# Attention followed by a three-way maximum layer on one core: the row maxima turned in five blocks of 116 columns in place of six of 96

## The chip, the cores and the metric

The kernel runs on 1 core of one Trainium2 chip. Its time is what the device takes for one execution, in microseconds (us). Before the change it was 1497.14 us, the median of 3 runs (1493.35 to 1499.3). A core has five engines that run side by side: TensorE (PE in the profile, with its weight loads shown apart as PEld), VectorE (DVE), ScalarE (ACT), GpSimd (POOL) and SyncE (SP), which issues DMA transfers.

## The reference

Everything is float32: 8 batches, 8 heads, 1152 keys, head size 64.

```python
q_pool = q.reshape(B, H, S // 2, 2, D).mean(axis=3)     # 576 queries
scores = scale * np.matmul(q_pool, k.transpose(0, 1, 3, 2))
scores = scores - np.max(scores, axis=-1, keepdims=True)
attn = np.exp(scores)
attn = attn / (np.sum(attn, axis=-1, keepdims=True) + 1e-09)
out = np.matmul(attn, v)
# x: 4608 tokens x 512, the heads of one token side by side
h = np.maximum(np.maximum(x @ w1, x @ w2), x @ w3)      # 4608 x 768
y = h @ w_out                                           # 4608 x 512
```

## The kernel before, in words

**Units.** The attention part is cut into 64 units, numbered 0 to 63: 8 batches, 4 pairs of heads, 2 halves of the queries. A unit holds 288 queries of each of two heads, 576 columns in all, side by side, against 1152 keys in 9 blocks of 128. Keys are on the partitions, queries along the columns.

**One unit, step by step.** For each of the 9 key blocks TensorE writes scores for both heads into `pqk` (L495 and L496, each half of a split float32 product), ScalarE copies them to the tile `s` (L501), and VectorE keeps a running maximum `acc`, 128 partitions x 2 heads x 288 queries (L507, L510). There are two score buffers, so the products of one block wait for the copy and the maximum of the block two before. The maximum of a query over the 128 partitions that are left is found per head: TensorE turns `acc` by three transposes of 96 columns into `pmt` (step "rows", L543), VectorE reduces that to `m`, 96 partitions x 3 (step "red", L549), and TensorE spreads `m` over all 128 partitions by three more transposes into `pmb` (step "bc", L556), 96 columns each. Per unit that makes six transposes of each sort. Then VectorE subtracts `pmb` from `s` in six instructions, one for each three key blocks and head (L571, 864 elements per partition), ScalarE takes the exponential of the same six pieces (L577), GpSimd adds the key blocks to `ksum` (L590, L592), and TensorE multiplies with the values into `pav` (L620) and sums the keys (L634, or L651 and L666 in units 0 to 15).

**The last layer.** The 4608 tokens are cut into nine chunks, most of 512 columns. A chunk is 216 matmuls into `ph` (L882, three matrices, each float32 product as three matmuls) and 72 into `po` (L937). Chunk 0 begins when the first batch is through and runs among the units of later batches. With it the weights, which come as 64-bit floats, are converted (tile `w64`, L782 to L815, mostly VectorE); the other chunks read the converted weights back. So units 0 to 8 have attention alone, those after them carry chunk 0 and conversions, and the later ones carry a steady share of chunks. The last two chunks and what is left of the one before run after the last unit.

**The order.** Nothing is scheduled at run time. Every step is put on a list with the engine it needs, what it must follow and a cost in us, such as `[pe(400)]` for the three transposes of "rows". The function `arrange` walks through a plan of time: whichever engine is free next takes, among the steps that are ready, the one with the lowest rank. The rank is the unit's number plus a number for the sort of step (table `RANK`) plus a number for the sort of step and the unit (table `NUDGE`, for names such as `sub.3`). What comes out is a fixed order of instructions on each engine, and semaphores hold an instruction until its inputs are there.

Of the kernel before, what the change touches and what calls it, by code (L numbers as in the profile page):

```python
# [9 lines left out]
F32 = mybir.dt.float32  # L10
# [12 lines left out]
QH = 288  # L23
DM = 512
# [11 lines left out]
    "qk": -64.087414,  # L36
    "cp": -201.632297,
    "mx": -98.140426,
    "rows": -272.840782,
    "red": -68.635955,  # L40
    "bc": -93.634816,
    "sub": 4.726236,
    "exp": -213.793739,
    "keys": -56.547354,
    "av": 20.056295,
    "xcopy": -255.632957,
    "psum": 357.906867,
    "eps": 37.531305,
    "inv": 376.584889,
    "xm": -67.169839,  # L50
    "load": -24.04249,
    "prep": 419.666386,
    "move": 224.230816,
    "split": 23.71928,
    "ffn": -28.691504,
    "rate": 0.892435,
    "mm": 52.75274,
    "fetch": -99.724728,
    "evac": -190.100398,
    "hhigh": 126.204061,  # L60
    "hlow": -167.886807,
    "conv": 378.084906,
    "rate0": 3.367239,
    "first_qk": 72.728419,
    "first_cp": -178.421168,
    "first_mx": 23.500417,
    "first_sub": 91.32154,
    "first_exp": 338.912979,
    "first_keys": 32.988795,
    "first_av": 60.682988,  # L70
    "first_xcopy": -140.422607,
    "first_psum": -82.473329,
    "first_inv": -18.571991,
    "first_xm": -117.084517,
    "first_load": -319.235449,
    "first_prep": -243.969765,
    "first_move": -391.229363,
    "first_split": 131.799961,
# [163 lines left out]
def pe(n):  # L242
    return ("pe", n * 1e-3)
# [15 lines left out]
def tile_attention_ffn(  # L259
# [214 lines left out]
    def scores(d, n, half):  # L474
# [7 lines left out]
        for kk in range(NK):  # L482
            apart = d < APART and kk % 3 == 2
            for hs in [(0, 1), (1, 2)] if apart else [(0, 2)]:
# [44 lines left out]
                if kk:  # L529
                    after = [c] + ([copies[0]] + (old.rows if old else []) if kk == 1 else [tops[-1]])  # L530
                    x = step("mx", r, [dve(n * QH)], top, after, give="ff" if apart else None)
                    tops.append(x)
                if not apart:
                    uses.append([c, x])

        o.rows, o.subs, o.exps, o.pt, o.pb, o.m = [], [[], []], {}, {}, {}, {}
        pools = (ps_a, ps_b)
        for h in range(2):

            def rows(e, h=h):  # L540
                o.pt[h] = pools[h].tile([P, 512], F32, tag="ab"[h], name=f"pmt{d}_{h}")
                for i in range(3):
                    nc.tensor.transpose(  # L543
                        o.pt[h][:96, i * P : (i + 1) * P], o.acc[:, h, 96 * i : 96 * i + 96], ident
                    )
# [476 lines left out]
```

## Time and profile before

| | us |
|---|---|
| median of 3 runs | 1497.14 |
| the profiled execution, its own time | 1492.46 |
| its span, first to last instruction | 1490.6 |
| PE busy | 1407.2 (94%) |
| POOL busy | 1076.9 (72%) |
| DVE busy | 1054.8 (71%) |
| ACT busy | 906.5 (61%) |

The profile shows one execution. "Busy" is the time in which an engine has an instruction under way; matmuls overlap and their ends are modelled, so the time by which one matmul holds up the next is read from how far the end of a run of them moves with each one more, not from the length of one. The granted TensorE clock (PEclk) is 1.00 where the chip grants 2.4 GHz and 0.50 where it grants 1.2 GHz; a stretch with some of both has a value in between.

### The profile page before, as it was taken

What the parts mean: (1) busy time and instruction counts of PE and PEld (TensorE: products, weight loads), DVE (VectorE), ACT (ScalarE), POOL (GpSimd) and SP (SyncE); (2) the same over time, 40 slices, a digit from 0 to 9 for tenths busy, and PEclk for the clock granted to TensorE, in tenths of its full rate; (3) what the DMA queues carried; (4) which work ended last, traced back from release to release, by engine and by line L of the source; (5) the groups of instructions that cost most, each with busy time, mean ns of one, the idle gap of its engine ahead of it and who ended that gap; (6) DMA issues with size and microseconds to landing.
All of it is one profiled execution on the core that took longest, in us unless ns stands there. A gap on an engine that the chain in (4) does not pass through costs nothing.

```text
span 1490.6 us, 24961 instructions
## 1 busy us (share of the span) xinstructions
PE 1407.2 (94%) x8832; PEld 1114.8 (75%) x8832; DVE 1054.8 (71%) x1441; ACT 906.5 (61%) x1464; POOL 1076.9 (72%) x835
## 2 busy tenths in 40 slices
PE   4889898897899999999999999999999999999999
PEld 4556676775777778777777877777777777778998
DVE  4798788898867777777678777777787778750110
ACT  4777656576666676667666776667667766641211
POOL 1888875689578887789978896788888978680210
PEclk9889899897799999999999999999999999999999
DMA  6565446574356755566466755665566546334441
GB/s 186 155 182 160 128 147 225 160 219 139 110 153 169 210 152 151 174 186 184 119 185 181 197 145 166 188 186 156 169 181 183 152 137 177 109 100 164 156 161 58
DMA packets 114763, 240.73 MB, mean 161 GB/s; under 512 B 15440, under 2 KB 75216, under 8 KB 114640
## 3 DMA queue, kind: packets, MB, share of 16 engines
q1 hardware_dynamic: 114064, 238.55, 54.7%
q8 instruction: 71, 1.16, 0.3%
q10 hardware_dynamic: 576, 0.59, 0.2%
q14 instruction: 52, 0.43, 0.1%
HBM read 144.70 MB, written 18.87 MB: 110 GB/s over the span
## 4 chain that ended last, share of the span: by engine, by line
PE 68%; POOL 2%; DVE 1%; DMA 1%; issue 1%; ACT 1%; SPq 0%; ACTq 0%; POOLq 0%
PE ph L882 26%; PE pav L620 12%; PE po L937 10%; PE pqk L495 7%; PE pqk L496 7%; PE pmt L543 2%; PE psum L634 2%; PE pmb L556 2%; POOL ksum L592 1%; DMA qq<-qraw 1%; DVE s L571 0%; DMA qraw<-in_qT_dram 0%; DVE acc L510 0%; DMA kraw<-in_kT_dram 0%; SPq L425 0%
## 5 line engine op out<-in xcount | busy, mean ns | idle before, releaser
L592 POOL TENSOR_TENSOR ksum<-ksum,s 128x576 f32<-128x576 f32 x448 | 638.0, 1424 | 25.2 <-ACT s L577 3.9
L882 PE MATMUL ph<-xh,w 128*128 128x512 f32 (+2 forms) x1440 | 458.4, 375 | 4.1 <-DVE w L815 2.4
L501 ACT COPY s<-pqk 128x576 f32<-128x576 f32 x576 | 360.8, 636 | 131.8 <-PE pqk L496 128.4
L495 PE MATMUL pqk<-qq,kc 128*128 128x288 f32 x1152 | 360.6, 329 | 57.7 <-DVE acc L510 35.3
L510 DVE TENSOR_TENSOR acc<-acc,pqk 128x576 f32<-128x576 f32 x448 | 334.2, 746 | 113.6 <-ACT s L501 110.7
L571 DVE TENSOR_TENSOR s<-s,pmb 128x864 f32<-128x864 f32 x384 | 393.1, 1045 | 11.2 <-PE pmb L556 11.2
L577 ACT ACTIVATE s<-s 128x864 f32<-128x864 f32 x384 | 352.2, 929 | 52.0 <-DVE s L571 48.4
L496 PE MATMUL pqk<-qq,kc 128*128 128x288 f32 x1152 | 334.2, 305 | 0.0
L495 PEld LDWEIGHTS pqk<-qq,kc 128*128 128x128 f32 x1152 | 226.9, 197 | 112.2 <-DVE acc L510 45.2
L620 PE MATMUL pav<-s,v 128*64 128x288 f32 x2304 | 305.7, 418 | 2.8 <-ACT s L577 2.6
L882 PEld LDWEIGHTS ph<-xh,w 128*128 128x128 f32 x1440 | 263.1, 188 | 42.7 <-issue 3.2
L882 PE MATMUL ph<-xl,w 128*128 128x512 f32 (+2 forms) x720 | 267.7, 372 | 0.0
L620 PEld LDWEIGHTS pav<-s,v 128*64 128x64 f32 x2304 | 166.3, 140 | 119.9 <-issue 14.6
L496 PEld LDWEIGHTS pqk<-qq,kc 128*128 128x128 f32 x1152 | 229.5, 199 | 10.1
L590 POOL TENSOR_TENSOR ksum<-s 128x576 f32<-128x576 f32 x64 | 91.9, 1436 | 134.8 <-ACT s L577 134.3
L913 POOL TENSOR_TENSOR h_lo<-hm,h_hi 128x512 fp32r<-128x512 f32 (+2 forms) x60 | 70.8, 1180 | 136.2 <-ACT h_hi L910 134.1
L903 DVE TENSOR_TENSOR hm<-hm,ph 128x512 f32<-128x512 f32 (+2 forms) x120 | 75.4, 629 | 127.9 <-PE ph L882 126.6
L549 DVE TENSOR_REDUCE m<-pmt 96x3 f32<-96x384 f32 x128 | 68.7, 551 | 108.5 <-PE pmt L543 108.3
L882 PEld LDWEIGHTS ph<-xl,w 128*128 128x128 f32 x720 | 135.8, 189 | 12.9
L391 POOL TENSOR_TENSOR kraw<-kraw 128x1152 fp32r<-128x1152 f32 x31 | 82.6, 2665 | 49.2 <-ACT kraw L387 48.6
L629 ACT COPY xr<-pav 128x288 f32<-128x288 f32 x64 | 25.5, 398 | 132.1 <-PE pav L620 131.9
L641 DVE RECIPROCAL rs<-rs 128x288 f32<-128x288 f32 (+1 forms) x64 | 96.4, 1506 | 9.4 <-ACT rs L638 8.9
(57 smaller groups left out, 1313.7 us busy)
## 6 DMA issues: line engine op xcount, KB each, us to landing
w<-w_split SPq DMA_DIRECT2D x144, 512.0 KB, 3.4
kc<-kraw SPq DMA_DIRECT2D x384, 96.0 KB, 2.6
qq<-qraw SPq DMA_DIRECT2D x252, 144.0 KB, 3.8
v<-in_vr_dram SPq DMA_DIRECT2D x32, 576.0 KB, 4.0
kraw<-in_kT_dram SPq DMA_DIRECT2D x31, 576.0 KB, 5.0
qraw<-in_qT_dram SPq DMA_DIRECT2D x31, 576.0 KB, 4.7
w<-in_win_dram SPq DMA_DIRECT2D x18, 512.0 KB, 5.5
w_split<-w SPq DMA_DIRECT2D x18, 512.0 KB, 4.4
```

Source lines behind the costliest of these rows:

```text
L495: nc.tensor.matmul(ps[:, h - hs[0], :QH], w, qq[:, 0, h], start=True, stop=False)
L496: nc.tensor.matmul(ps[:, h - hs[0], :QH], w, qq[:, 1, h], start=False, stop=True)
L501: nc.scalar.copy(o.s[kk // 3][:, kk % 3, slice(*hs)], o.ps[kk, hs][:, :, :QH])
L510: nc.vector.tensor_tensor(acc, acc, ps, op=ALU.max)
L571: nc.vector.tensor_tensor(s, s, o.pb[h][:, None, :QH].broadcast_to([P, 3, QH]), op=ALU.subtract)
L577: nc.scalar.activation(s, s, AF.Exp, scale=SCALE)
L590: vec[e].tensor_tensor(o.ksum, o.s[0][:, 0], x, op=ALU.add)
L592: vec[e].tensor_tensor(o.ksum, o.ksum, x, op=ALU.add)
L620: nc.tensor.matmul(o.pav[64 * h : 64 * h + 64, :QH], pr.v[:, kk, h], o.s[kk // 3][:, kk % 3, h], start=(kk == 0), stop=(kk == NK - 1),)
L641: nc.vector.reciprocal(o.rs, o.rs)
L882: nc.tensor.matmul(t.ps[:, : hi - lo], w[:, a, kk], xx[:, kk, lo:hi], start=(kk == 0 and i == 0), stop=(kk == 3 and i == 2),)
L937: nc.tensor.matmul(t.ps[:, : hi - lo], ww[:, kk, ms], hh[:, kk, lo:hi], start=(kk == 0 and i == 0), stop=(kk == 5 and i == 2),)
```

## The change

The 576 columns of a unit are no longer turned head by head. With the two heads side by side as one row of 576 columns, they are turned in five blocks of 116 columns that start 115 columns apart, so that neighbours share one column (5 x 115 + 1 = 576). The first three blocks go to the first PSUM bank (tile `pmt_0`, then `pmb_0`), the last two to the second. The reduction of a bank makes three or two maxima for each of 116 partitions. The subtraction and the exponential follow the banks: of each three key blocks the first piece covers columns 0 to 344 of the row (3 x 345 = 1035 elements) and the second columns 345 to 575 (3 x 231 = 693), where before each covered a head (3 x 288 = 864). Costs in the plan are changed to fit, those of the last layer's matmuls too, and all numbers of `RANK` and `NUDGE` are new, so the whole order of the program is made anew. Which engine does a step is as before, and no other instruction is added or taken away.

```diff
+CB = 115
...
-    "qk": -64.087414,
+    "qk": -94.8622,
...
         pools = (ps_a, ps_b)
-        for h in range(2):
-
-            def rows(e, h=h):
+        for h, (x0, x1) in enumerate([(0, 3 * CB), (3 * CB, 2 * QH)]):
+            nb, w = 3 - h, x1 - x0
+
+            def rows(e, h=h, nb=nb, x0=x0):
                 o.pt[h] = pools[h].tile([P, 512], F32, tag="ab"[h], name=f"pmt{d}_{h}")
-                for i in range(3):
+                acc = o.acc.rearrange("p h q -> p (h q)")[:, x0:]
+                for i in range(nb):
                     nc.tensor.transpose(
-                        o.pt[h][:96, i * P : (i + 1) * P], o.acc[:, h, 96 * i : 96 * i + 96], ident
+                        o.pt[h][: CB + 1, i * P : (i + 1) * P], acc[:, CB * i : CB * i + CB + 1], ident
                     )
...
-                o.m[h] = small.tile([96, 3], F32, tag=f"m{h}", name=f"m{d}_{h}")
+                o.m[h] = small.tile([CB + 1, 3], F32, tag=f"m{h}", name=f"m{d}_{h}")
...
-                        o.pb[h][:, 96 * i : 96 * i + 96],
-                        o.m[h][:, i : i + 1].broadcast_to([96, P]),
-                        ident[:96, :96],
+                        o.pb[h][:, CB * i : CB * i + CB + 1],
+                        o.m[h][:, i : i + 1].broadcast_to([CB + 1, P]),
+                        ident[: CB + 1, : CB + 1],
...
-            x = step("rows", d + 0.1 * h, [pe(400)], rows, [tops[-1], gone] + (old.subs[h] if old else []))
+            x = step("rows", d + 0.1 * h, [pe(133 * nb)], rows, [tops[-1], gone] + (old.subs[h] if old else []))
             o.rows.append(x)
-            x = step("red", d, [("dve", 0.467)], reduce, [x])
-            b = step("bc", d + 0.1 * h, [pe(335)], bcast, [x])
+            x = step("red", d, [("dve", 0.067 + nb * 0.133)], reduce, [x])
+            b = step("bc", d + 0.1 * h, [pe(89 + 99 * nb)], bcast, [x])
...
-                def sub(e, i=i, h=h):
-                    s = o.s[i][:, :, h]
+                def sub(e, i=i, h=h, x0=x0, x1=x1, w=w):
+                    s = o.s[i].rearrange("p k h q -> p k (h q)")[:, :, x0:x1]
                     nc.vector.tensor_tensor(
-                        s, s, o.pb[h][:, None, :QH].broadcast_to([P, 3, QH]), op=ALU.subtract
+                        s, s, o.pb[h][:, None, :w].broadcast_to([P, 3, w]), op=ALU.subtract
                     )
...
-                o.exps[i, h] = step("exp", r, [("act", 0.829)], exp, [x])
+                o.exps[i, h] = step("exp", r, [("act", 0.109 + w / 400)], exp, [x])
...
-                            "mm", at, n, [pe(45 + 1.236 * m)], product,
+                            "mm", at, n, [pe(14 + 1.326 * m)], product,
```

The order shows the change at three places. On TensorE in the middle of the program (unit 39 in both), where the transposes stand among the score products of the next unit, before:

```order
L543 MATMUL pmt_0_8212<-ident,acc_8052 96x128 x3
L495 MATMUL pqk_0_8218<-qq_0_7996,kc_0_7848 128x288
L496 MATMUL pqk_0_8218<-qq_0_7996,kc_0_7848 128x288
L495 MATMUL pqk_0_8218<-qq_0_7996,kc_0_7848 128x288
L496 MATMUL pqk_0_8218<-qq_0_7996,kc_0_7848 128x288
L543 MATMUL pmt_1_8225<-ident,acc_8052 96x128 x3
L495 MATMUL pqk_1_8231<-qq_0_7996,kc_0_7848 128x288
L496 MATMUL pqk_1_8231<-qq_0_7996,kc_0_7848 128x288
L495 MATMUL pqk_1_8231<-qq_0_7996,kc_0_7848 128x288
L496 MATMUL pqk_1_8231<-qq_0_7996,kc_0_7848 128x288
L556 MATMUL pmb_0_8239<-ident,m_0_8223 128x96 x3
```

and after:

```order
L589 MATMUL pmt_0_8192<-ident,acc_8022 116x128 x3
L538 MATMUL pqk_0_8197<-qq_0_7940,kc_0_7855 128x288
L539 MATMUL pqk_0_8197<-qq_0_7940,kc_0_7855 128x288
L538 MATMUL pqk_0_8197<-qq_0_7940,kc_0_7855 128x288
L539 MATMUL pqk_0_8197<-qq_0_7940,kc_0_7855 128x288
L589 MATMUL pmt_1_8205<-ident,acc_8022 116x128 x2
L538 MATMUL pqk_1_8210<-qq_0_7940,kc_0_7855 128x288
L539 MATMUL pqk_1_8210<-qq_0_7940,kc_0_7855 128x288
L538 MATMUL pqk_1_8210<-qq_0_7940,kc_0_7855 128x288
L539 MATMUL pqk_1_8210<-qq_0_7940,kc_0_7855 128x288
L605 MATMUL pmb_0_8217<-ident,m_0_8203 128x116 x3
```

The places are the same; the second group has two transposes in place of three, and the blocks are wider.

On VectorE near the beginning, the subtractions of unit 3 (`s_0_538` in the program before, `s_0_547` in the one after) and the running maxima of the unit after it (`acc_815` and `acc_778`; `w` are the conversions), before:

```order
L815 TENSOR_TENSOR w_1_692<-w_1_256_720,w_105 128x256
L571 TENSOR_TENSOR s_0_538<-s_0_538,pmb_0_750 128x3x288
L571 TENSOR_TENSOR s_0_538<-s_0_538,pmb_1_756 128x3x288
L571 TENSOR_TENSOR s_1_610<-s_1_610,pmb_0_750 128x3x288
L571 TENSOR_TENSOR s_1_610<-s_1_610,pmb_1_756 128x3x288
L571 TENSOR_TENSOR s_2_670<-s_2_670,pmb_0_750 128x3x288
L571 TENSOR_TENSOR s_2_670<-s_2_670,pmb_1_756 128x3x288
L785 TENSOR_SCALAR w_105<-w_2_0_776 128x512
L507 TENSOR_TENSOR acc_815<-s_0_794,pqk_1_740 128x576
```

and after:

```order
L550 TENSOR_TENSOR acc_778<-s_0_723,pqk_1_756 128x576
L620 TENSOR_TENSOR s_0_547<-s_0_547,pmb_0_770 128x3x345
L724 TENSOR_TENSOR xr<-xr,psum_731 128x288
L553 TENSOR_TENSOR acc_778<-acc_778,pqk_2_763 128x576
L620 TENSOR_TENSOR s_0_547<-s_0_547,pmb_1_775 128x3x231
L553 TENSOR_TENSOR acc_778<-acc_778,pqk_3_787 128x576
L620 TENSOR_TENSOR s_1_619<-s_1_619,pmb_0_770 128x3x345
L620 TENSOR_TENSOR s_1_619<-s_1_619,pmb_1_775 128x3x231
L620 TENSOR_TENSOR s_2_658<-s_2_658,pmb_0_770 128x3x345
L553 TENSOR_TENSOR acc_778<-acc_778,pqk_4_816 128x576
L620 TENSOR_TENSOR s_2_658<-s_2_658,pmb_1_775 128x3x231
```

Before, all six stand in one run ahead of the first maximum; now maxima stand between them.

The third place is the last conversion on VectorE (`wo_lo` is the second part of the last weight matrix). The number behind `acc` is the unit, before:

```order
L510 TENSOR_TENSOR acc17_3530<-acc17_3530,pqk17_5_3626 128x576
L675 TENSOR_TENSOR xr_106<-xr_106,psum15_3538 128x288
L510 TENSOR_TENSOR acc17_3530<-acc17_3530,pqk17_6_3635 128x576
L815 TENSOR_TENSOR wo_lo_104<-w64_23_256_3621,w64_105 128x256
L510 TENSOR_TENSOR acc17_3530<-acc17_3530,pqk17_7_3658 128x576
```

and after:

```order
L861 TENSOR_TENSOR w64_23_256_3922<-w64_23_256_3922,wo_hi_103 128x256
L864 TENSOR_TENSOR wo_lo_104<-w64_23_0_3849,w64_105 128x256
L864 TENSOR_TENSOR wo_lo_104<-w64_23_256_3922,w64_105 128x256
L595 TENSOR_REDUCE m19_0_3954<-pmt19_0_3942 116x3
L595 TENSOR_REDUCE m19_1_3967<-pmt19_1_3956 116x2
```

The last conversion stood among the maxima of unit 17 and stands at the end of those of unit 19: the conversions reach over two units more.

## Rows read from the trace of the kernel before

**Rows 1.** Stretches of the span: us, busy of each engine (count), granted clock, DMA.
```profile
core 0: us, PE busy (x) PEld busy (x) DVE busy (x) ACT busy (x) POOL busy (x), PEclk, DMA share, GB/s
0.00:40.00 40.00, 20.91 (x82) 16.51 (x83) 18.10 (x29) 17.92 (x27) 9.38 (x12) 0.96 0.67 182
40.00:160.00 120.00, 100.05 (x708) 72.73 (x706) 100.91 (x156) 85.33 (x134) 102.36 (x74) 0.91 0.59 167
160.00:400.00 240.00, 207.04 (x1298) 158.53 (x1298) 204.24 (x360) 148.01 (x251) 175.12 (x135) 0.87 0.55 160
400.00:1320.00 920.00, 912.31 (x5729) 712.79 (x5728) 704.52 (x856) 619.66 (x977) 747.59 (x571) 1.00 0.58 166
1320.00:1490.60 170.60, 166.87 (x1022) 154.26 (x1020) 26.99 (x44) 35.55 (x78) 42.42 (x46) 1.00 0.39 132
```

**Rows 2.** The chain that ended last, shares of the span by engine (page).
```profile
PE 68%; POOL 2%; DVE 1%; DMA 1%; issue 1%; ACT 1%; SPq 0%; ACTq 0%; POOLq 0%
```

**Rows 3.** PE's waits: 0 to 160 us, then 160 to 400 us (in total, times, longest).
```profile
PE pqk L495 <- DVE acc L510: 19.2, 17, 3.5
...
PE pqk L495 <- DVE acc L510: 11.9, 13, 2.8
```

**Rows 4.** A run of `pmt` transposes in the steady stretch: one, two, three of it.
```profile
606.46 0.32 PE L543 MATMUL pmt<-ident,acc 128*96 128x128 f32 x1 [0.87 <-ACT xr L629]
606.46 0.43 PE L543 MATMUL pmt<-ident,acc 128*96 128x128 f32 x2 [0.87 <-ACT xr L629]
606.46 0.54 PE L543 MATMUL pmt<-ident,acc 128*96 128x128 f32 x3 [0.87 <-ACT xr L629]
```

**Rows 5.** A run of `pmb` transposes likewise.
```profile
606.83 0.25 PE L556 MATMUL pmb<-ident,m 96*128 96x96 f32 x1
606.83 0.33 PE L556 MATMUL pmb<-ident,m 96*128 96x96 f32 x2
606.83 0.41 PE L556 MATMUL pmb<-ident,m 96*128 96x96 f32 x3
```

**Rows 6.** Groups by line and shape: busy us, mean ns of one, idle before.
```profile
L571 DVE TENSOR_TENSOR s<-s,pmb 128x864 f32<-128x864 f32 x384 | 393.1, 1045 | 11.2 <-PE pmb L556 11.2
L577 ACT ACTIVATE s<-s 128x864 f32<-128x864 f32 x384 | 352.2, 929 | 52.0 <-DVE s L571 48.4
L549 DVE TENSOR_REDUCE m<-pmt 96x3 f32<-96x384 f32 x128 | 68.7, 551 | 108.5 <-PE pmt L543 108.3
L543 PE MATMUL pmt<-ident,acc 128*96 128x128 f32 x384 | 62.2, 283 | 9.4 <-ACT xr L629 5.3 <-DVE acc L510 3.9
L556 PE MATMUL pmb<-ident,m 96*128 96x96 f32 x384 | 51.0, 252 | 0.4 <-DVE m L549 0.3
L556 PEld LDWEIGHTS pmb<-ident,m 96*128 96x128 f32 x384 | 42.7, 139 | 6.6 <-DVE m L549 1.4 <-DVE acc L507 1.3 <-issue 1.3
L543 PEld LDWEIGHTS pmt<-ident,acc 128*96 128x96 f32 x384 | 42.4, 128 | 32.0 <-issue 14.9 <-ACT xr L629 7.5 <-DVE acc L510 4.4
```

**Rows 7.** Subtractions near the beginning, and PE's score products behind them.
```profile
71.09 3.94 DVE L571 TENSOR_TENSOR s<-s,pmb 128x864 f32<-128x864 f32 x4
75.75 0.61 PE L495 MATMUL pqk<-qq,kc 128*128 128x288 f32 x1 [3.51 <-DVE acc L510]
86.37 5.86 DVE L571 TENSOR_TENSOR s<-s,pmb 128x864 f32<-128x864 f32 x6
91.19 0.40 PE L495 MATMUL pqk<-qq,kc 128*128 128x288 f32 x1 [2.49 <-ACT s L501]
```

**Rows 8.** Stretches cut at units, columns as Rows 1: attention alone, four; late conversions, three.
```profile
92.80:156.40 63.60, 57.02 (x428) 41.25 (x424) 53.26 (x85) 45.80 (x74) 53.72 (x41) 0.97 0.55 152
327.90:400.80 72.90, 57.24 (x347) 44.93 (x344) 61.10 (x108) 44.38 (x81) 53.06 (x46) 0.77 0.46 125
```

More of the change, by code (lines that the diff above doesn't have):

```diff
@@ L35 @@
 RANK = {
-    "qk": -64.087414,
[L37 to L78, printed above, removed]
+    "qk": -94.8622,
+    "cp": -198.877,
+    "mx": -110.1936,
+    "rows": -297.5399,
+    "red": -97.7108,
+    "bc": -69.2978,
+    "sub": 36.0255,
+    "exp": -154.9623,
+    "keys": -14.5562,
+    "av": 14.8431,
+    "xcopy": -242.7422,
+    "psum": 306.6745,
+    "eps": 163.4791,
+    "inv": 411.5164,
+    "xm": -165.8669,
+    "load": 11.9358,
+    "prep": 513.6605,
+    "move": 372.9744,
+    "split": 31.5471,
+    "ffn": -33.8173,
+    "rate": 1.0394,
+    "mm": 49.1178,
+    "fetch": -156.7626,
+    "evac": -234.7904,
+    "hhigh": 172.1589,
+    "hlow": -152.0307,
+    "conv": 478.2091,
+    "rate0": 4.4379,
+    "first_qk": 87.3127,
+    "first_cp": -260.4178,
+    "first_mx": 25.0784,
+    "first_sub": 35.563,
+    "first_exp": 326.0935,
+    "first_keys": -44.827,
+    "first_av": 37.0199,
+    "first_xcopy": -183.8483,
+    "first_psum": -32.0782,
+    "first_inv": -61.85,
+    "first_xm": -117.3451,
+    "first_load": -320.6766,
+    "first_prep": -184.3904,
+    "first_move": -506.8185,
+    "first_split": 49.1161,
 }
 NUDGE = {
[35 rows of a table removed]
[77 rows of a table added]
 }
@@ L545, in rows, with reduce @@
                     )
-            def reduce(e, h=h):
-                o.m[h] = small.tile([96, 3], F32, tag=f"m{h}", name=f"m{d}_{h}")
+            def reduce(e, h=h, nb=nb):
+                o.m[h] = small.tile([CB + 1, 3], F32, tag=f"m{h}", name=f"m{d}_{h}")
                 nc.vector.tensor_reduce(
-                    o.m[h], o.pt[h][:96, : 3 * P].rearrange("p (t k) -> p t k", t=3), axis=AX.X, op=ALU.max
+                    o.m[h][:, :nb],
+                    o.pt[h][: CB + 1, : nb * P].rearrange("p (t k) -> p t k", t=nb),
+                    axis=AX.X,
+                    op=ALU.max,
@@ L551, in reduce, with bcast @@
                 )
-            def bcast(e, h=h):
+            def bcast(e, h=h, nb=nb):
                 o.pb[h] = pools[h].tile([P, 512], F32, tag="ab"[h], name=f"pmb{d}_{h}")
-                for i in range(3):
+                for i in range(nb):
                     nc.tensor.transpose(
-                        o.pb[h][:, 96 * i : 96 * i + 96],
-                        o.m[h][:, i : i + 1].broadcast_to([96, P]),
-                        ident[:96, :96],
+                        o.pb[h][:, CB * i : CB * i + CB + 1],
+                        o.m[h][:, i : i + 1].broadcast_to([CB + 1, P]),
+                        ident[: CB + 1, : CB + 1],
@@ L573, in sub, with exp @@
                     )
-                def exp(e, i=i, h=h):
-                    s = o.s[i][:, :, h]
+                def exp(e, i=i, x0=x0, x1=x1):
+                    s = o.s[i].rearrange("p k h q -> p k (h q)")[:, :, x0:x1]
                     nc.scalar.activation(s, s, AF.Exp, scale=SCALE)
                 r = d + 0.1 * i + 0.05 * h
-                x = step("sub", r, [dve(3 * QH)], sub, [b, copies[-1]])
+                x = step("sub", r, [dve(3 * w)], sub, [b, copies[-1]])
                 o.subs[h].append(x)
-                o.exps[i, h] = step("exp", r, [("act", 0.829)], exp, [x])
+                o.exps[i, h] = step("exp", r, [("act", 0.109 + w / 400)], exp, [x])
@@ L945, in ffn @@
                     tail[0] = ffn_step(
-                        "mm", at, n, [pe(45 + 1.236 * w)], product, [tail[0]] + (hdone if kk == 0 else []),
+                        "mm", at, n, [pe(14 + 1.326 * w)], product, [tail[0]] + (hdone if kk == 0 else []),
                         take="ff" if kk == 0 else None, cols=3 * w,
```

112 rows, old and new, of the table NUDGE are left out of this document.

## The prediction, made before the changed kernel ran

> **What bounds the kernel now.** I first read the stretches [rows 1]. From 400 to 1320 us TensorE is busy 912.31 of 920 us at a granted clock of 1.00, and from 1320 us to the end 166.87 of 170.6; VectorE, next in that middle stretch, is busy 704.52. There only less TensorE work, or a shorter wait of TensorE, can shorten the program. From 40 to 400 us it is otherwise: TensorE is busy 307 of 360 us, so 53 us idle, its granted clock is 0.91 and then 0.87, and VectorE is busy 305. This stretch holds the units with attention alone, which have nothing to fill TensorE, and the weight conversions, which load VectorE. The chain that ended last says the same in short: 68% of it is TensorE's, 1% VectorE's [rows 2]. Then I asked what TensorE waits for in the early stretch: score products that wait for the running maximum, 19.2 us up to 160 us and 11.9 us up to 400 us [rows 3]. So the reader should see two programs: a late one (about 45 of the 64 units, and the tail) in which each TensorE nanosecond counts, and an early one in which TensorE, VectorE and the order share the blame.
>
> **The change, part by part.** The sum is made against the profiled execution: 1492.46 us, of which 1490.6 is span. It is 4.7 us below the median of the three runs (1497.14), so I add 4.7 at the end. "No change" means within 0.5%, about 7.5 us, which is what a measurement of this kernel can tell.
>
> *Turning the maxima.* A unit has six transposes `pmt` now and will have five. What one more costs is read from a run of them: it ends 0.32, 0.43, 0.54 us after it begins with one, two, three, so 0.11 us each [rows 4]. (The mean length, 283 ns, would overstate it, and the group's busy time, 62.2/384 = 0.16 us, holds part of the first one's latency [rows 6].) The moving operand stays the 128-column identity, so the pace should stay: minus 0.11 us per unit.
>
> *Spreading them.* Six `pmb` at a pace of (0.41 - 0.25)/2 = 0.08 us [rows 5] become five with 116 moving columns in place of 96. No row shows 116, but two rows enclose it: 0.08 at 96 columns and 0.11 at 128. In between by columns it is 0.08 + 20/32 x 0.03 = 0.10. Six at 0.08 are 0.48, five at 0.10 are 0.50: plus 0.02. The ends are 5 x 0.08 = 0.40 (minus 0.08) and 5 x 0.11 = 0.55 (plus 0.07).
>
> Together a unit gets 0.09 us of TensorE work shorter, between 0.19 and 0.04. Over 64 units that is 5.8 us, between 12 and 2.6.
>
> *Reduction.* 128 reductions take 551 ns each over 384 elements [rows 6]. The second one of each unit will have 256. By elements alone it loses 551/3 = 184 ns; if a part of the 551 ns is fixed, less, and at least nothing. I take 0.13 us, 8.5 us of VectorE in all. In the steady stretch that is hidden, since VectorE idles there for over 200 of 920 us. In the early stretch VectorE is busy 305 of 360 us; for its 18 units 18 x 0.13 = 2.3 us may show, but the same units' TensorE saving (18 x 0.09 = 1.6) lies in the same time. I count the larger of the two and so add 0.7. Total so far minus 6.5.
>
> *Subtraction and exponential by banks.* Counts stay (384 each), elements too: 1035 + 693 = 2 x 864. At 1045 and 929 ns per 864 elements [rows 6] the first piece gets at most a fifth longer (about 0.2 us) and the second as much shorter, so the last exponential of a unit, on which the value product waits, ends where it did. Nothing, as long as the second piece comes last; if the first piece of the last bank came last the loss were 0.2 + 0.2 us in the units where TensorE waits for it, and in the steady stretch its idle time, 7.7 us for all causes, shows that it rarely waits for anything.
>
> *The order.* In the steady stretch the places are as before: transposes among the next unit's score products, then last-layer matmuls between. In the early stretch two things move, with opposite signs. First, six subtractions of unit 3 that stood in one run now have maxima between them. Before, a run of four took 3.94 us and the next score product came after 3.51 us of idle TensorE; a run of six took 5.86 us and 2.49 us of idle followed [rows 7]. Of the 31.1 us of waits for the maximum [rows 3] the program before has eight runs of three or more among its first 20 units, four of them of four to six, and the one after has three, one of them of five: if those of four to six that go, three, give back 2.5 us each and the two shorter ones 1 us each, that is about 10 us. This is the upper end, because VectorE was already full there, and work that moves out of the run is done elsewhere. Second, the last conversion moves from unit 17 to unit 19, and chunk 0 starts one unit later. So one more unit is spent with attention alone and one more among thin conversions. The first sort costs little: four such units lasted 63.6 us with 6.6 us idle, 1.6 us each [rows 8]. Of the second sort three lasted 72.9 us with 15.7 us idle, 5.2 us each, and their granted clock was 0.77, so that of 19.1 us busy some 4.4 were lost to the clock [rows 8]. That is at most 1.6 + 5.2 + 4.4 = 11 us, and nothing where VectorE's idle time (11.8 us in the three) takes up the spread. Between a gain of 10 and a loss of 11 I take a gain of 3: the runs are gone for certain, while the longer lead matters only if VectorE does no better per unit than before.
>
> Sum: 1492.46 - 6.5 - 3 = 1483 us as the profiled execution counts, 1487.7 as the runs count. I say 1487.5 us, 0.64% less.
>
> **Rivals.**
> 1. *The weight load sets the pace.* A `pmt` loads 96 weight columns now and will load 116. Its load takes 128 ns [rows 6]; in proportion to the columns it becomes 155 ns, and if that, not the 0.11 us, became the spacing, five would take 0.775 in place of 0.66 us: plus 0.115, with `pmb` plus 0.135 us a unit, 8.6 us in all, and no gain of the order: 1501 on the profile's count, 1506 on the runs'. Slower, and it decides as soon as the spacing is above 0.13 us. Against it: the loads of `pmb`, of 128 columns, take 139 ns and yet those transposes follow each other in 0.08 us [rows 5, 6], so loads run ahead of one another. 7 in 100. The Trainium skill ("TensorE: Matmul & The Clock Gate", section "LDWEIGHTS (loading the stationary operand)") has a load grow with its columns and not with its rows, P/1.2 ns, which is 80 ns for 96 columns and an estimated 97 ns for 116; the trace's 128 ns for 96 does not agree with the figure, and no run here yet shows whether the growth is there.
> 2. *The longer lead costs its full 11 us.* VectorE's idle time per unit stays, the two units are simply added, and the runs that were broken up give nothing: 1492.46 - 6.5 + 11 = 1497, 1501.7 on the runs' count. For it speaks that the runs before had VectorE full, so that breaking them up frees none of its time. 18 in 100.
> 3. *The saving alone, or less.* The two effects of the order cancel, or the transposes save their lower 2.6 us: 1492.46 minus 2.6 to 6.5, so 1486 to 1490, 1490.7 to 1494.5 on the runs' count, within 0.5%. 25 in 100.
> 4. *The order gives all 10 us*, and TensorE stays filled: 1492.46 - 6.5 - 10 = 1476, 1480.7 on the runs' count. It is the far end of my forecast.
>
> **How the numbers follow.** The forecast, with the order's gain anywhere from 1 to 10 us, gets 50 in 100 and 1480 to 1490 us as its own range. A time below 1489.7 us is faster by over 0.5%: nearly all of the forecast and a little of the third rival, 0.51. Above 1504.6 us is slower by over 0.5%: most of the first rival, and the part of the second in which the lead costs more than the early rows show or in which the median does not sit 4.7 above the profile, 0.13. Within 0.5%: 0.36. The range that should hold 8 in 10 reaches from below the forecast, where `pmb` costs 0.08 us a piece (another 6 us) or the order gives its all, 1474, to the second rival, 1502.
>
> **What the profile after would show.** Right: 320 `pmt` and 320 `pmb`; a run of two or three `pmt` still spaced by 0.11 us and one of `pmb` by 0.10; in a stretch of the same units in the middle TensorE as full as now and each unit about 0.09 us shorter; reductions of two lengths, the shorter by some 0.13 us; fewer and shorter waits of score products for the maximum before 400 us. Wrong: a spacing of `pmt` near 0.155 us; more than 53 us of idle TensorE ahead of the steady stretch, or a lower granted clock in it; a steady stretch in which TensorE waits for exponentials or maxima. The step that I trust least is the order's 3 us.

## The result, and the profile after

| | before | after |
|---|---|---|
| median of the runs, us | 1497.49 (4 runs, 1493.35 to 1499.3) | 1482.68 (4 runs, 1480.85 to 1483.04) |
| ratio | 1 | 0.9893, 95% interval 0.9875 to 0.9911 |
| profiled execution, own time / span, us | 1492.46 / 1490.6 | 1483.04 / 1480.9 |
| PE busy, us | 1407.2 | 1400.6 |
| time at the lower granted clock, us (from the trace; mean granted clock 0.969 and 0.975) | 93 | 73 |

The kernel is 14.8 us (1.1%) faster; 1487.5 was forecast. As profiled executions count, the forecast was 1483 and the profile shows 1483.04. The 4.7 us that I added for the median were not owed by the new kernel: its runs lie close together, and its profile, the slowest of them, is 0.4 us above their median. As differences the two counts part: the sum gave 9.5 us less, the profiles show 9.4, but the medians show 14.8 (13.3 to 18.7 by the interval). The profile of before was a quick execution of its kernel: of the 99 runs of it that were made beside the experiments, 8 were at 1492.46 us or below.

The stretches of the kernel after, to be held against [rows 1]:

```profile
0.00:40.00 40.00, 20.87 (x80) 16.37 (x81) 17.91 (x28) 17.68 (x27) 9.24 (x12) 0.96 0.67 182
40.00:160.00 120.00, 101.28 (x706) 72.51 (x705) 99.88 (x156) 85.64 (x134) 102.60 (x73) 0.91 0.59 167
160.00:400.00 240.00, 208.75 (x1329) 154.06 (x1329) 207.19 (x360) 158.35 (x264) 187.33 (x142) 0.92 0.57 167
400.00:1320.00 920.00, 912.16 (x5609) 708.47 (x5608) 692.36 (x855) 609.48 (x973) 737.60 (x567) 1.00 0.58 167
1320.00:1480.90 160.90, 157.56 (x986) 146.92 (x984) 28.80 (x46) 33.38 (x69) 41.92 (x44) 1.00 0.37 125
```

From 160 to 400 us more matmuls fit (1329 against 1298), at a granted clock of 0.92 against 0.87; from 40 to 400 us TensorE idles 50.0 us against 53. The middle is as full as before. The chain of the page [rows 2] has a little more of VectorE:

```profile
PE 70%; DVE 4%; DMA 2%; issue 1%; POOL 1%; ACT 1%; SPq 0%; ACTq 0%; DVEq 0%
```

The runs of transposes of the kernel after, one, two and three of them, as [rows 4, 5]:

```profile
581.15 0.27 PE L589 MATMUL pmt<-ident,acc 128*116 128x128 f32 x1
581.15 0.38 PE L589 MATMUL pmt<-ident,acc 128*116 128x128 f32 x2
581.15 0.49 PE L589 MATMUL pmt<-ident,acc 128*116 128x128 f32 x3
582.71 0.26 PE L605 MATMUL pmb<-ident,m 116*128 116x116 f32 x1
582.71 0.36 PE L605 MATMUL pmb<-ident,m 116*128 116x116 f32 x2
582.71 0.46 PE L605 MATMUL pmb<-ident,m 116*128 116x116 f32 x3
```

`pmt` is still spaced by 0.11 us, and `pmb` at 116 columns by 0.10: the two figures of the forecast. Its groups by shape, against [rows 6]:

```profile
L620 DVE TENSOR_TENSOR s<-s,pmb 128x1035 f32<-128x1035 f32 x192 | 235.2, 1229 | 45.4 <-PE pmb L605 45.4
L620 DVE TENSOR_TENSOR s<-s,pmb 128x693 f32<-128x693 f32 x192 | 166.6, 870 | 0.5 <-PE pmb L605 0.5
L595 DVE TENSOR_REDUCE m<-pmt 116x3 f32<-116x384 f32 x64 | 35.5, 555 | 81.2 <-PE pmt L589 81.1
L595 DVE TENSOR_REDUCE m<-pmt 116x2 f32<-116x256 f32 x64 | 26.9, 420 | 10.7 <-PE pmt L589 10.7
L605 PE MATMUL pmb<-ident,m 116*128 116x116 f32 x320 | 51.3, 267 | 0.8 <-DVE m L595 0.8
L605 PEld LDWEIGHTS pmb<-ident,m 116*128 116x128 f32 x320 | 38.5, 137 | 7.0 <-issue 3.9 <-DVE m L595 2.2
L589 PEld LDWEIGHTS pmt<-ident,acc 128*116 128x116 f32 x320 | 36.5, 136 | 33.9 <-issue 14.9 <-ACT xr L678 6.7 <-DVE acc L553 5.1
```

There are 320 of each sort, the second reduction is 0.135 us shorter (0.13 forecast), and the load of a wider `pmt` takes 136 ns in place of 128. TensorE's waits for the running maximum, 0 to 160 and then 160 to 400 us, against [rows 3]:

```profile
PE pqk L538 <- DVE acc L553: 16.4, 15, 2.9
...
PE pqk L538 <- DVE acc L553: 15.7, 22, 1.7
```

They come to 32.1 us, where they were 31.1. So the runs of subtractions [rows 7] are broken up, single waits after 160 us are shorter (at most 1.7 us, was 2.8), but there are more of them. The gain is not there.

### The profile page after: what moved, and what is told of

Read it like the earlier page. It is cut to its first block, busy times and chain, and to the rows that moved or that the text cites. A ratio compares the mean times of both kernels' runs of the same rounds, so it can differ in the third digit from the quotient of the medians.

```text
span 1480.9 us, 24740 instructions
## 1 busy us (share of the span) xinstructions
PE 1400.6 (95%) x8704; PEld 1098.3 (74%) x8704; DVE 1046.1 (71%) x1441; ACT 904.5 (61%) x1464; POOL 1078.7 (73%) x835
## 4 chain that ended last, share of the span: by engine, by line
PE 70%; DVE 4%; DMA 2%; issue 1%; POOL 1%; ACT 1%; SPq 0%; ACTq 0%; DVEq 0%
PE ph L931 27%; PE pav L669 13%; PE po L986 10%; PE pqk L538 7%; PE pqk L539 7%; PE pmt L589 2%; PE psum L683 2%; PE pmb L605 2%; DVE acc L553 1%; DMA w<-in_wout_dram 1%; DVE s L620 1%; DMA qq<-qraw 1%; POOL ksum L641 0%; DVE w L834 0%; DVE w L839 0%
## 5 line engine op out<-in xcount | busy, mean ns | idle before, releaser
L931 PE MATMUL ph<-xh,w 128*128 128x512 f32 (+2 forms) x1440 | 464.6, 377 | 5.4 <-DVE hm L952 4.0
L620 DVE TENSOR_TENSOR s<-s,pmb 128x1035 f32<-128x1035 f32 (+1 forms) x384 | 396.9, 1049 | 46.0 <-PE pmb L605 46.0
L626 ACT ACTIVATE s<-s 128x1035 f32<-128x1035 f32 (+1 forms) x384 | 354.8, 934 | 60.2 <-DVE s L620 57.1
L595 DVE TENSOR_REDUCE m<-pmt 116x3 f32<-116x384 f32 (+1 forms) x128 | 61.1, 488 | 91.9 <-PE pmt L589 91.9
```

The source lines that it names most:

```text
L620: nc.vector.tensor_tensor(s, s, o.pb[h][:, None, :w].broadcast_to([P, 3, w]), op=ALU.subtract)
L626: nc.scalar.activation(s, s, AF.Exp, scale=SCALE)
L931: nc.tensor.matmul(t.ps[:, : hi - lo], w[:, a, kk], xx[:, kk, lo:hi], start=(kk == 0 and i == 0), stop=(kk == 3 and i == 2),)
```

## The experiments

The change has two halves, the layout of the blocks and the order. I ran each on the other's partner. "Old order" and "new order" are the exact sequences of instructions before and after on every engine (the transposes that a layout lacks or has more aside); only the layout differs within a family. Each ratio is against runs of the kernel before on the same chip, whose medians were 1495.81 to 1497.47 us.

**Five blocks in the old order.** The layout of after with the tables and costs of before:

```diff
-    "qk": -94.8622,
+    "qk": -64.087414,
...
-            x = step("rows", d + 0.1 * h, [pe(133 * nb)], rows, [tops[-1], gone] + (old.subs[h] if old else []))
+            x = step("rows", d + 0.1 * h, [pe(400)], rows, [tops[-1], gone] + (old.subs[h] if old else []))
```

> The five blocks of 116 columns, with every instruction at the place it has in the program before (the plan keeps the old tables and costs). Theory A (both parts pay: 0.09 us of TensorE per unit, the rest of the measured 14.8 us from the order): 6.5 us below before, about 1491 us, between 1485 and 1495. Theory B (the layout's saving is hidden, the order made all of it): as before, 1497 us. Theory C (the layout made all of it): 1483 us.

Measured: 1495.9 us, ratio 1.0002 (0.9986 to 1.0018). The layout alone brings nothing.

**Six blocks in the new order.** The layout of before with the tables and costs of after:

```diff
-    "qk": -64.087414,
+    "qk": -94.8622,
...
-            x = step("red", d, [("dve", 0.467)], reduce, [x])
+            x = step("red", d, [("dve", 0.067 + (3 - h) * 0.133)], reduce, [x])
```

> Six blocks of 96 columns and pieces by heads, with every instruction at the place it has in the changed program. Theory A: 6.5 us above the changed kernel, about 1489 us, 8 us below before. Theory B: as the changed kernel, 1483 us. Theory C: as before, 1497 us.

Measured: 1494.96 us, ratio 0.9988 (0.9975 to 1.0002). The order alone brings 1.8 us, which its interval does not part from nothing. A, B and C all fall: the halves give 0.02% and -0.12%, the two together -1.07%. What is over and above their sum is 0.97% of the time, 14.5 us, give or take 4 (the intervals joined as independent).

**New order, last block turned twice**, so six `pmt` again:

```diff
-                for i in range(nb):
...
+                for i in range(3):
+                    c = CB * min(i, nb - 1)
+                    nc.tensor.transpose(o.pt[h][: CB + 1, i * P : (i + 1) * P], acc[:, c : c + CB + 1], ident)
```

> The changed kernel with a sixth transpose per unit put back: the last block is turned twice, into a part of the bank that nobody reads; order unchanged. Theory A and C: 64 x 0.11 = 7 us above the changed kernel, about 1490 us, with 0.11 us a unit in the steady stretch. Theory B (TensorE's work is hidden): as the changed kernel, 1483 us.

Measured: 1486.08 us, ratio 0.9928 (0.9907 to 0.995). That is 5.2 us above the changed kernel by the ratios, give or take 4, nearer to A and C than to B. Their 0.11 us a unit does not show in the steady stretch: of 41 x 0.11 = 4.5 us the traces below have 1.8.

**The same, and the second reduction over three blocks:**

```diff
-                    o.m[h][:, :nb],
-                    o.pt[h][: CB + 1, : nb * P].rearrange("p (t k) -> p t k", t=nb),
+                    o.m[h],
+                    o.pt[h][: CB + 1, : 3 * P].rearrange("p (t k) -> p t k", t=3),
```

> As the run with the sixth transpose, and the second reduction of a unit also reads the third block, as long as the first (about 0.13 us more of VectorE per unit, 8.5 us in all). Theory A: at most 2.3 us above the run with the sixth transpose, in the early units alone, about 1491 us. Rival (VectorE's work counts in all units): 8 us above it, 1498 us.

Measured: 1490.01 us, ratio 0.9948 (0.993 to 0.9966). These runs stood beside those with the sixth transpose on one chip, 3.9 us above them, and the fastest of the ten (1487.46) is slower than the slowest of the six (1486.66). So the longer reduction costs a few us in this order; that is too little for the rival's 8, and does not rule out A's 2.3.

**The pieces of subtraction and exponential.** Next I suspected that each order suits the pieces that it was made for (even ones of 288 columns, uneven ones of 345 and 231). So four kernels take the other pieces. Even pieces on five blocks, in the old and in the new order:

```diff
-                    s = o.s[i].rearrange("p k h q -> p k (h q)")[:, :, x0:x1]
...
+                    s = o.s[i][:, :, h]
+                    top = o.pb[h][:, None, : 1 if h else QH].broadcast_to([P, 3, QH])
```

> Old order, five blocks, but subtraction and exponential in even pieces of 288 columns as before (the second piece subtracts the first maximum of its bank from all its columns, so the shift is wrong and the work is the same). Theory T1 (each order suits the pieces it was planned for; in the old order the longer first piece of 345 columns delays the maxima and ate the layout's saving): 5 to 7 us below before, about 1490 us. Theory T2 (in the old order TensorE's saving is taken up by other waits whatever the pieces are): as before and as the five blocks in the old order, 1496 us.

Measured: 1494.2 us, ratio 0.9983 (0.9968 to 0.9999).

> New order, five blocks, even pieces. T1: above the changed kernel by what even pieces cost the new order, 1488 us. T2: as the changed kernel, 1483 us.

Measured: 1482.42 us, ratio 0.9898 (0.9876 to 0.992). Uneven pieces on six blocks, in the new and in the old order:

```diff
-                    s = o.s[i][:, :, h]
...
+                x0, x1 = ((0, 345), (345, 2 * QH))[h]
...
+                    top = o.pb[h][:, None, : x1 - x0 if h else 1].broadcast_to([P, 3, x1 - x0])
```

> New order, six blocks of 96, but subtraction and exponential in uneven pieces of 345 and 231 columns (the first piece subtracts the first maximum of its bank from all its columns; same work, wrong shift). T1 (the even pieces cost the new order 5 to 6 us): 1489 us, 6.5 us above the changed kernel for TensorE's work. T2: 1495 us, as six blocks in the new order with even pieces.

Measured: 1495.28 us, ratio 0.9988 (0.9973 to 1.0004).

> Old order, six blocks, uneven pieces. T1: above before by what the pieces cost the old order, 1502 us. T2: as before, 1496 us.

Measured: 1498.29 us, ratio 1.001 (0.9997 to 1.0024). By the ratios the pieces move the time by 2.8 us in the old order with five blocks and by 1.5 or less in the other three: T1, which asked for 5 us or more each time, falls.

**Old order, last block turned twice** (the edit of the sixth `pmt` above on five blocks in the old order):

> Five blocks in the order before, with the last block of a unit turned twice, so that TensorE again has six transposes pmt per unit; nothing else differs. Theory T2 (in the order before, the time that the second group of transposes no longer takes is spent by the next score product waiting for its buffer, which ScalarE's copy or VectorE's first maximum frees): the sixth transpose fills that wait, so 1495 to 1498 us, the same as without it (1495.9), and the waits of score products for copies and maxima in the steady stretch fall back to about those of before. Rival, the sum as forecast (each ns of TensorE counts there, and something else costs the five blocks 6 us in this order): 64 x 0.11 = 7 us more, 1503 us.

Measured: 1496.09 us, ratio 0.9987 (0.9971 to 1.0003). As T2 says, and not the rival's 1503. But the waits did not fall back: in the stretch of the traces below the weight loads of score products wait 15.6 us under "issue" and 2.4 us for VectorE's first maximum, against 15.3 and 2.7 with five blocks and 11.9 and 2.2 in the kernel before. T2's number came out, its reason for this transpose did not.

**The kernel before with a shorter second reduction:**

```diff
-                    o.m[h], o.pt[h][:96, : 3 * P].rearrange("p (t k) -> p t k", t=3), axis=AX.X, op=ALU.max
+                    o.m[h][:, : 3 - h],
+                    o.pt[h][:96, : (3 - h) * P].rearrange("p (t k) -> p t k", t=3 - h),
...
-                        o.m[h][:, i : i + 1].broadcast_to([96, P]),
+                        o.m[h][:, min(i, 2 - h) : min(i, 2 - h) + 1].broadcast_to([96, P]),
```

> The kernel before, its order and its six transposes, but the second reduction of each unit covers two of its three blocks and the third block takes the maxima of the second (this leaves out the maxima of 96 queries of each unit; the work of the other engines is the same). VectorE has 0.13 us less per unit. Theory V (VectorE's shorter reduction is worth about 4 us in the first 20 units whatever the order): 1492 to 1493 us, with the first 20 units 3 to 5 us shorter. Theory T2 (in the order before, one part's saving is taken up by the next wait): 1495 to 1497, the same as before. The sum as forecast (2.3 us at most in the early units): 1494.5 to 1496.

Measured: 1495.03 us, ratio 0.9984 (0.9967 to 1.0002). The median lies in the ranges of T2 and of the sum, and the interval does not rule out V's 4 us. V's own sign is missing: in the profile the first 20 units are not 3 to 5 us shorter (442.8 us, before 441.7).

**All six of each sort on the wide blocks**, turned, reduced and spread as often as before; first in the old order, then in the new (the edits of the sixth turn and of the longer reduction, and this one):

```diff
-                for i in range(nb):
+                for i in range(3):
+                    c = CB * i + (i >= nb)
...
-                        o.pb[h][:, CB * i : CB * i + CB + 1],
+                        o.pb[h][:, c : c + CB + 1],
```

> The order before with blocks of 116 columns and banks, but the last block turned, reduced and spread twice, so that all counts are those of before (six pmt, a second reduction over three blocks, six pmb) and only the width of the blocks and the split of the pieces differ. TensorE has 6 x 0.10 + 6 x 0.11 us here against 6 x 0.083 + 6 x 0.11 before, 0.11 us a unit more. Theory T2 (in the order before, what TensorE saves or adds here is taken up by other waits): 1495 to 1498 us, as before. Rival, the sum as forecast (each ns of TensorE counts for the later 45 units at least): 5 to 7 us more than before, 1501 to 1504. Theory W (the widths themselves cost the five blocks their gain in this order, by what the blocks do to the waits of the score products): 1500 or more, and the sixth of each sort taken away gives back its share.

Measured: 1501.95 us, ratio 1.004 (1.0021 to 1.0059). T2 as a rule for the whole old order falls: wider blocks cost nearly what their spacing says. The rival and W both hold this number.

> The kernel after, its order, with the last block turned, reduced and spread twice: the counts of before on the layout of after. It differs from the kernel that turned it and reduced it twice (1490.0) by one spread transpose of 116 columns per unit, 64 x 0.10 = 6.4 us if each ns counts, 3 us if it counts as the sixth turn did (3.4 of 7.0). Theory A2 (in the new order the counts of small work are what the layout is worth, the widths nothing): 1493 to 1496 us, as the layout before had in this order (1495.0). Theory W2 (the layout before is slow in this order for another reason, such as its widths or where its turns wait for ScalarE's copy xr): 1490 to 1492.5, clearly below 1495.

Measured: 1498.12 us, ratio 1.0005 (0.9989 to 1.002). A2's side: the counts of small work carry the gain, and one spread transpose more costs 8.5 us, give or take 4.

With these two there is a ladder from the old layout to the new in each order. The steps in us, from the ratios times 1497 (an error of 3 to 4 us on each), beside what TensorE's spacings give over 64 units:

| step | by spacing | old order | new order |
|---|---|---|---|
| blocks 116 wide, six of each (0.02 us x 6) | +7.7 | +6.0 | +2.5 |
| a spread less (0.10 us) | -6.4 | -7.9, with the next row | -8.5 |
| a shorter second reduction (VectorE) | 0 | | -3.0 |
| a turn less (0.11 us) | -7.0 | +2.2 | -5.2 |
| sum | -5.7 | +0.3 | -14.2 |

And the profiled executions, cut where the first maxima of units 20 and 61 begin (within an order the work of a stretch is the same; across orders it is not, since the new one carries more of the last layer in the middle):

| us | to unit 20 | unit 20 to 61 | unit 61 to the end |
|---|---|---|---|
| old order: before | 441.7 | 817.3 | 231.6 |
| all six, wide | 448.1 | 820.0 | 231.8 |
| sixth turn | 443.3 | 819.9 | 231.7 |
| five blocks | 443.2 | 816.8 | 231.4 |
| new order: six blocks of before | 427.3 | 848.0 | 218.4 |
| all six, wide | 422.7 | 849.8 | 218.4 |
| sixth turn and full reduction | 427.1 | 843.0 | 218.0 |
| sixth turn | 424.0 | 842.5 | 218.0 |
| after | 422.7 | 840.6 | 217.6 |

The middle has a mean granted clock of 1.00 in all of them; only two, before and the sixth turn in the old order, have 3.4 us at 0.50 in it. Kernels that differ only in their pieces differ there by 1.3 us at most, so steps of a few us can be read. Ahead of unit 20 such kernels differ by up to 5.0 us (before 441.7, with uneven pieces 446.7), so there they can't.

From six wide blocks to five, spacing says 41 x 0.21 = 8.6 us less in the middle. In the new order 9.2 arrive, in the old one 3.2. From the six narrow blocks of before to five it says 41 x 0.09 = 3.7: 7.4 arrive in the new order, 0.5 in the old. Neither order gives what spacing says, and the steps do so least: a spread less gives 6.8 us in the new order and 0.1 in the old (4.1 by spacing), a turn less 1.8 and 3.1 (4.5 by spacing; the 0.1 and the 3.1 share a profile with a stretch of lower clock, see below).

What the old order keeps back shows in the weight loads' waits of the middle (total us, times, longest), first with all six:

```profile
448.13:1268.12 819.99, 812.57 (x5094) 634.20 (x5093) 627.11 (x761) 554.49 (x877) 674.38 (x519) 1.00 0.58 170
PEld pqk L496 <- issue: 14.0, 37, 1.1
PEld pmt L548 <- issue: 12.7, 29, 0.4
PEld pqk L496 <- DVE acc L511: 4.8, 8, 1.5
...
PEld pqk L496 <- DVE acc L508: 0.3, 2, 0.2
```

and with the spread (and the third block of the second reduction) gone:

```profile
443.34:1263.24 819.90, 812.17 (x5053) 630.61 (x5051) 621.98 (x761) 554.97 (x877) 675.19 (x519) 1.00 0.58 170
PEld pqk L496 <- issue: 15.6, 37, 1.5
PEld pmt L548 <- issue: 12.7, 29, 0.4
PEld pqk L496 <- DVE acc L511: 4.9, 6, 1.5
PEld pqk L496 <- DVE acc L508: 2.4, 11, 0.3
```

and with five blocks:

```profile
443.17:1259.99 816.82, 807.83 (x5011) 624.99 (x5010) 622.67 (x760) 554.64 (x877) 674.46 (x519) 1.00 0.59 171
PEld pqk L496 <- issue: 15.3, 37, 1.2
PEld pqk L496 <- DVE acc L511: 5.1, 10, 1.5
PEld pqk L496 <- DVE acc L508: 2.7, 11, 0.4
PEld pqk L496 <- ACT s L502: 1.8, 3, 1.1
```

With the spread gone, 41 transposes are gone (5094 to 5053 matmuls) and the stretch is as long. The loads of score products wait 11 times and 2.4 us for VectorE's first maximum of a unit (L508), where it was twice and 0.3 us, and 1.6 us more under "issue". But this step is not all waits: its profile alone has this stretch of lower clock,

```profile
868.20:871.60 3.40, 2.97 (x9) 2.59 (x10) 3.40 (x5) 2.63 (x5) 3.40 (x4) 0.50 0.51 163
```

and there it falls back by 1.3 us against all six: counted from unit 20 its first maxima are 2.0 us earlier at unit 41 and 0.7 at unit 42. So the 0.1 us of this step is in part an accident of one execution. All six against five, neither with such a stretch, is the better pair: 5.4 of the 8.6 us are missing, and the loads of score products wait 2.4 us more for the first maximum, 1.3 more under "issue" and 1.2 more for ScalarE's copy (L502; 0.6 us with all six). Whether each of these waits held up its matmul by as much is not shown. TensorE's busy time does not show them: it falls by 4.7 us (812.57 to 807.83), where the spacing of what was taken away is 8.6, since the modelled end of one matmul covers a short wait of the next.

In the new order the spread, taken away, takes a wait with it. All six, and then the spread gone (both stretches end 1.0 us ahead of unit 61):

```profile
422.68:1271.48 848.80, 844.21 (x5222) 660.30 (x5221) 629.24 (x763) 556.51 (x883) 678.95 (x521) 1.00 0.57 167
PE pmt L590 <- ACT xr L678: 4.5, 6, 1.5
PEld pmt L590 <- ACT xr L678: 6.2, 7, 1.8
PEld pqk L538 <- DVE acc L553: 3.7, 11, 0.6
```

```profile
427.11:1269.12 842.01, 840.30 (x5182) 655.59 (x5181) 629.17 (x763) 555.24 (x883) 679.81 (x521) 1.00 0.58 169
PE pmt L590 <- ACT xr L677: 1.3, 3, 0.6
PEld pmt L590 <- ACT xr L677: 2.4, 4, 0.8
PEld pqk L538 <- DVE acc L553: 4.9, 14, 0.7
```

The stretch is 6.8 us shorter: TensorE's busy time falls by 3.9 us, about the 41 x 0.10 = 4.1 of the spacing, and its idle time by 2.9 (4.6 to 1.7). That idle time is nearly all turns waiting for ScalarE's copy `xr`, which frees their bank, 1.3 us in place of 4.5: two such waits, of 1.2 and 1.5 us in units 35 and 43, are gone. This comes back in other executions: in the new order the three kernels with six spreads wait 4.4 (six blocks of before), 7.1 (the same with uneven pieces) and 4.5 us there, the four with five spreads 1.2 to 3.0.

## Why the forecast held, and which steps did not

The time was forecast rightly, 4.8 us too high and well within the range, but not all of its working stands, and part of the agreement is luck.

- *Spacings.* Right: 0.11 and 0.10 us. Rival 1 is out: the load of a wider `pmt` grew by 8 ns and did not set the pace.
- *Reduction.* Its size was right (0.135 us), its worth too small. I let it bring at most 2.3 us and hid most of that behind TensorE's saving, so that the sum has 0.7. Giving it back costs 3.9 us in the new order (1490.01 against 1486.08 on one chip), so 0.7 is too little there. Where the time goes is not shown: the profiles have 3.1 us ahead of unit 20, where kernels that differ only in their pieces are as far apart, and 0.6 in the middle.
- *Subtraction and exponential by banks.* Right: even pieces in the new order give 1482.42 us against 1482.68.
- *"Each TensorE nanosecond counts" in the later part.* This is the step that failed. The layout was to give 0.09 us in each unit there, and in the middle it gives 0.01 in the old order (0.5 us over 41 units) and 0.18 in the new (7.4 us), with TensorE equally busy. I took a busy share of 99% for proof that nothing else is late, so that the waits could not change. They do: in the old order loads of score products wait longer for buffers when the transposes ahead of them are fewer, in the new order the turns wait less for `xr`.
- *The order.* I gave it 3 us of its own. Alone it has 1.8 (between 3.7 less and 0.3 more), so 3 is not ruled out, but its reason is: broken runs of subtractions should have shortened the waits for the maximum, and these are 32.1 us against 31.1. Rival 2 is out too: the lead is a unit longer, but the order alone does not cost 11 us. With five blocks the order is worth 16.3 us (from ratio 1.0002 to 0.9893), a term that the sum does not have.
- *Adding them.* Saving and order were summed as if independent. Alone they give +0.3 and -1.8 us, together 14.8 less. That the sum met the profile (1483 against 1483.04) is luck: each term, put into the old kernel alone, is smaller than forecast, what the two give only together makes up for it, and the profile that the sum starts from is a quick one, so that a sum of 9.5 us less ended where a gain of 14.8 in the medians did.

What stays open: the middle explains 6.9 of the 14.5 us (0.3 against -14.2) by which the layout is worth more in the new order (-7.4 against -0.5). Most of the rest lies ahead of unit 20 (-4.6 against +1.5 in the profiles). There, one profile of each kernel does not tell which wait takes the saving. The granted clock does not settle it: up to unit 20 it is 0.90 with six blocks in the new order and 0.92 in the kernel after, but 0.91 with even pieces, whose stretch is as short (422.0 us). Runs of one kernel differ by more than the steps (before: 1489 to 1504 us over all its runs, after: 1481 to 1483 in four); in which part of the program, and why the few runs of the new kernel lie closer together, is not shown. That the turn is worth less in the old order rests on the medians (+2.2 against -5.2); the profiles have 3.5 us less for it in both, and I don't call it shown. No version tried beats the kernel after; even pieces are its equal.

## What to carry to other kernels

A saving on the busiest engine is worth its nanoseconds only where the next instruction's inputs and buffers are ready that much earlier, and it is worth more where it takes a wait away; look at the starts and the loads' waits behind the shortened step, not at the busy share. When a change comes with a new order, run each half with the other's old partner: here both halves alone gave nothing that shows, and dropping either for that would have lost the 15 us. Repeating one small operation without use, one at a time, gives a ladder that prices each step in its own place.

## What the runs showed of the hardware that was not expected

A float32 transpose with 128 moving columns follows the one before in 0.11 us whether 96 or 116 weight columns are loaded; with the moving columns at 96 and 116 it is 0.08 and 0.10 us (all in stretches with a granted clock of 1.00). The load itself took 128 ns for 96 columns and 136 for 116, as means over the whole program. The Trainium skill ("TensorE: Matmul & The Clock Gate", section "LDWEIGHTS (loading the stationary operand)") has it grow as P/1.2 ns, an estimated 17 ns for these 20 columns; the trace shows 8.
